# One list for the whole of an attention and MoE kernel: the source orders every engine's work

## The chip, the core and the metric

The kernel runs on one core of one Trainium2 chip. A core has five engines that run side by side, each with its own stream of instructions in a fixed order: TensorE (PE) multiplies matrices, VectorE (DVE), ScalarE (ACT) and GpSimd (POOL) compute element by element, and SyncE (SP) issues most of the DMA transfers. An instruction starts when its engine has finished the ones ahead of it and when the semaphores that it waits for are set; whatever stands behind a waiting instruction on its engine waits too. The metric is the device time of one execution in microseconds (us).

## The reference

Attention over 9 blocks of 64 positions, where a position sees its own block and those before it, and then a feed-forward layer with a squared ReLU on the 4608 tokens of all 8 batches:

```python
def _attn_ref(q, k, v):                      # each (8, 8, 576, 64): batch, head, position, width
    scale = 1.0 / np.sqrt(D)
    scores = scale * np.matmul(q, k.transpose(0, 1, 3, 2))
    mask = block_i >= block_j                # blocks of 64 positions
    scores = np.where(mask, scores, -1000000000.0)
    scores = scores - np.max(scores, axis=-1, keepdims=True)
    attn = np.exp(scores)
    attn = attn / (np.sum(attn, axis=-1, keepdims=True) + 1e-09)
    return np.matmul(attn, v).astype(np.float32)

def _moe_ref(x, w_in, w_out):                # (4608, 512), (512, 2048), (2048, 512)
    h = x @ w_in
    r = np.maximum(h, 0.0)
    return ((r * r) @ w_out).astype(np.float32)
```

All inputs and outputs are fp32. Most matmuls of the kernel run on pairs of fp16 numbers: each operand is scaled by a power of two and split into a high half and the remainder (the low half), and a product is the sum of three matmuls, high by high, high by low and low by high.

## The kernel before

**Attention.** Work is cut into 40 *passes*; most names carry batch, head pair and a number of a row group, so `px_4_2_0_0` is a value product of batch 4, head pair 2. Two heads are always worked on together. Passes 0 to 7 are the rows 0 to 2 of the blocks of batches 0 and 1 (G_X), passes 8 to 15 are rows 3 to 8 of the same (G_Y), and passes 16 to 39 are all rows of batches 2 to 7 (G_XY, three score groups each). Passes 0 to 15 take their scores from fp32 matmuls. The rest first run a *front* (passes 12 to 15 only its part on v): the sums of |q|, |k| and |v| on ACT, two small matmuls (`pm`) that bring the maximum to all partitions, the scales on DVE, and then the split of q and k on ACT and DVE (`qs`, `k1`, and `k2` with the halves swapped), which three DMA transposes turn into `qT` and `kT`. A score group is a set of matmuls into `ps`, a running maximum on DVE, the exponential on ACT (`p32`), its sum on POOL, the reciprocal on DVE, and the scaled split into `p_rows` (high half on ACT, low half on DVE). DMA transposes turn `p_rows` into `p_turned`; in passes 0 to 11 matmuls into `pt` and a copy do it, and the copies of passes 8 to 11 alternate between ACT and DVE (constant EV). The value matmuls (`px`) multiply `p_turned` by the split `v16`, and ACT writes the result to `x32`.

**MoE.** When all head pairs of a batch's rows are there, the norm of the tokens is formed, and x is scaled and split into `xt`. Twelve *chunks* of 384 tokens follow, in the order 0, 1, 2, 4, 3, 5, 7, 6, 8, 10, 9, 11. A chunk has 16 *units*: 12 matmuls into `ph`, then Relu out of PSUM into `r` on ACT, Square of `r` in place on ACT, the cast of `r` to `hidden`'s high half on DVE, and the remainder on DVE (in chunk 0 mostly on POOL). Then come 3 outputs of 48 matmuls each into `po`, a scaling into `ob` on DVE and the transfer to HBM. `ph` and `po` share a ring of 2 PSUM buffers, `r` has 3 buffers, the score groups 2, and `px`, `pm`, `pt` and the norms 2 together.

**What sets the order.** A class `Queue` stands around each engine. Its line 93 issues every instruction of the kernel, so all groups of the profile have line L93 (L96 after the change) and are told apart by their tiles' names. While `nc.held` is set, `Queue` makes each instruction depend on the one before it on its engine, and so the order in which the source calls them is the order on the engine. Otherwise the tile framework's own scheduler chooses the order from its own simulation.

The *head* of the program (the weights, passes 0 to 11, the norms that chunk 0 needs and the 16 units of chunk 0) is ordered by the class `Plan`, called from `plan_head`. Each task has an engine, a duration in ns, the tasks that it comes after, a rank, and the buffer rings that it takes and frees. `run` simulates the engines: among the tasks that can start on the engine that is free first it takes, within LOOK = 300 ns (100 for ranks of 80 and over), the one with the lowest rank, and calls its function at once, with `nc.held` set. The time of a transfer is 1800 ns plus its bytes at 375 per ns on one wire.

The *body* (passes 12 to 39 and everything else of the MoE) is written by generators in program order, and the framework's scheduler orders it. `one_pass` writes a score group with `softmax`, then pours a number of MoE steps (`pour`, `fill`) that FILL gives per pass, for instance:

```python
            softmax(t, group, ready_rows)
            for g in parts:
                defer(DELAY[0], finish, t, g)
            pour(rate / ng / 2)
            if gi == 0 and i + 1 < len(passes):
                front(passes[i + 1])
```

A step is one unit (`moe_in`) or a quarter of an output (`moe_out`, 12 matmuls). `defer` puts value matmuls off by DELAY[0] = 14 steps, a norm by 6, and `hurry` writes them earlier where a buffer is needed again. The front of a pass is written behind the first score group of the pass before it.

Of the kernel before, what the change touches and what calls it, by code (L numbers as in the profile page):

```python
# [44 lines left out]
EV = ("ACT", "DVE")  # L45
SPIN = 5
NQ_CK = 1
W_FIX = 112
DELAY = (14, 6, 1)
FILL = (14, 6, 7, 7, 10, 10, 9, 7)  # L50
# [4 lines left out]
N0 = 60  # L55
LOADS = "p0 p1 r0 p2 r1 r2 p3 r3 r4 r5 r6 r7 r8 r9 r10 r11 r12 r13 Y0 r14 r15 Y1 z0 z1 z2 z3 z4 z5 z6"
# [64 lines left out]
class Plan:  # L121
# [7 lines left out]
    def add(self, name, queue, ns, after, rank, make, takes=(), frees=(), size=0):  # L129
        assert name not in self.tasks, name  # L130
        self.tasks[name] = (queue, ns, after, rank, make, takes, size)
        for owner, ring in frees:
            self.holders.setdefault((owner, ring), []).append(name)

    def run(self):
# [3 lines left out]
        end, issued, taken = {}, {}, {r: [] for r in self.rings}  # L139
        left = list(tasks)  # L140

        def ready(name):
            queue, _, after, _, _, takes, _ = tasks[name]
            needs = list(after)
            for ring in takes:
                if len(taken[ring]) >= self.rings[ring]:
                    needs += self.holders[taken[ring][-self.rings[ring]], ring]
            if any(n not in end for n in needs):
                return None
            at = [issued[n] if tasks[n][0] == queue else end[n] + self.LAG[tasks[n][0]] for n in needs]  # L150
            return max([free[queue]] + at)

        while left:
            times = [(ready(n), tasks[n][3], n) for n in left]
            times = [x for x in times if x[0] is not None]
            if not times:
                raise RuntimeError(f"stuck: {left[:40]}")
            first = min(times)
            queue = tasks[first[2]][0]
            at, _, name = min(  # L160
                (x for x in times if tasks[x[2]][0] == queue and x[0] <= first[0] + (LOOK if x[1] < 80 else 100)), key=lambda x: (x[1], x[0])
            )
            queue, ns, _, _, make, takes, size = tasks[name]
            left.remove(name)
            for ring in takes:
                taken[ring].append(name)
            free[queue] = at + ns
            end[name] = at + ns
            issued[name] = at + ns + 60
            if size:  # L170
                wire = max(wire, at + 1800) + size / 375
                end[name] = wire
            make()

@with_exitstack
def attention_moe_kernel(ctx: ExitStack, tc: tile.TileContext, qk1, v1, qkt, qk, vm, vt, w_in, w_out, out):
# [101 lines left out]

    def pow2_of_max(st, n, name):

        turned, largest, spread, read = pow2_steps(st, n, name)
        turned()
        largest()
        spread()
        return read()
# [144 lines left out]
    def front(t):  # L430

        u, c = t["u"], t["chunks"]
        if t["whole"]:
            t["es"] = D**-0.5
            return
        v32 = t["v32"][:, :, 0:c, :]
        st = small.tile([P, 3], F32, tag="st", name=f"st_{u}")
        a = 2 if t["native"] else 0
        if not t["native"]:
            raw = t["raw"]  # L440
            qs = p1.tile([P, NJ, P], F16, tag="qs", name=f"qs_{u}")
            k1 = p1.tile([P, NJ, P], F16, tag="k1", name=f"k1_{u}")
            k2 = p1.tile([P, NJ, P], F16, tag="k2", name=f"k2_{u}")
            q3 = raw[:, 0].rearrange("p (j d) -> p j d", d=D)
            k3 = raw[:, 1].rearrange("p (j d) -> p j d", d=D)
            nc.scalar.activation(k1[:, :, 0:D], k3, AF.Abs, accum_out=st[:, 1:2])
            nc.scalar.activation(qs[:, :, 0:D], q3, AF.Abs, accum_out=st[:, 0:1])
        else:
            k2 = p1.tile([P, NJ, P], F16, tag="k2", name=f"k2_{u}")
        rest = k2.rearrange("p j d -> p (j d)")[:, 0 : 10 * D].rearrange("p (h c d) -> p h c d", h=2, d=D)  # L450
        nc.scalar.activation(rest[:, :, 0:c, :], v32, AF.Abs, accum_out=st[:, 2:3])
        m = pow2_of_max(st[:, a:3], 3 - a, u)
        s = scale_of(m, A_ATT, 3 - a, u)
        xsc = small.tile([P, 1], F32, tag="xsc", name=f"xsc_{u}")
        nc.vector.tensor_scalar(xsc, m[:, 2 - a : 3 - a], 2.0 ** (-A_ATT - A_P), None, op0=ALU.mult)
        t["xsc"] = xsc
        if t["native"]:
            t["es"] = D**-0.5
        else:
            es = t["es"] = small.tile([P, 1], F32, tag="es", name=f"es_{u}")  # L460
            nc.vector.tensor_scalar(
                es, m[:, 0:1], m[:, 1:2], -(2.0 ** (-2 * A_ATT)) * D**-0.5, op0=ALU.mult, op1=ALU.mult
            )
            nc.scalar.activation(k1[:, :, 0:D], k3, AF.Copy, scale=s[:, 1:2])
            nc.scalar.activation(qs[:, :, 0:D], q3, AF.Copy, scale=s[:, 0:1])
            nc.vector.scalar_tensor_tensor(
                k1[:, :, D:P], k3, s[:, 1:2], k1[:, :, 0:D], op0=ALU.mult, op1=ALU.subtract
            )
            nc.vector.scalar_tensor_tensor(
                qs[:, :, D:P], q3, s[:, 0:1], qs[:, :, 0:D], op0=ALU.mult, op1=ALU.subtract  # L470
            )
            pairs = [k.bitcast(I32).rearrange("p j (z d) -> p j z d", z=2) for k in (k1, k2)]
# [798 lines left out]
```

## Time and profile before

| what | us |
|---|---|
| median of 3 runs (lowest to highest) | 1064.48 (1063.92 to 1066.38) |
| the profiled execution | 1065.6 |
| its span, first to last instruction | 1063.8 |
| busy: PE / DVE / ACT / POOL | 1014.8 / 714.1 / 645.4 / 82.1 |
| `ph` matmuls, 2304, busy | 407.4 |
| `po` matmuls, 1728, busy | 386.7 |
| first `ph` matmul starts at | 38.81 |
| mean granted TensorE clock | 0.989 of full speed |

The page's first part gives busy time, share of the span and count of each engine (PEld is TensorE's weight load, which runs beside the matmuls). Busy times of matmuls overlap, since they are pipelined: a `ph` matmul has a mean of 331 ns though they follow each other faster. A group of instructions reads as line, engine, operation, output<-input, tile shapes, count, then busy time and mean ns of one, then the engine's idle time just before them and what ended it. A row of the timeline gives start, length, the instructions in a run (x12 is twelve of them), and in brackets an idle time before it with what ended it. A row of the table by stretch gives the stretch, its length, busy time and count of the five engines in the order PE, PEld, DVE, ACT, POOL, and then the granted clock, the busy share of the DMA engines and GB/s.

### The profile page before, as it was taken

Reading aid. Unit: us, or ns where it says so; the run is one execution under the profiler, and the core shown is the slowest. Engines: PE = TensorE matmul, PEld = TensorE weight load, DVE = VectorE, ACT = ScalarE, POOL = GpSimd, SP = SyncE. Lnnn points to the kernel's source line nnn. Section 1 sums busy time; section 2 is a strip of 40 time slices with the busy share of each in tenths; the row PEclk is TensorE's granted clock in tenths of the full one; section 3 lists DMA queues with packets and bytes.
Section 4 is the critical chain, followed back from the end, with each engine's and each line's share of the span. In section 5 each row is a group of like instructions: output and inputs, shape, how many; then the busy total and the mean of one; then the engine's idle time right before and its main releaser. Section 6 shows DMA issues by size and latency. Waiting matters only on the chain.

```text
span 1063.8 us, 18829 instructions
## 1 busy us (share of the span) xinstructions
PE 1014.8 (95%) x6867; PEld 535.7 (50%) x6867; DVE 714.1 (67%) x1942; ACT 645.4 (61%) x1636; POOL 82.1 (8%) x182
## 2 busy tenths in 40 slices
PE   7688999999999999998999999999999999999998
PEld 6344434544554555454455455455455555455553
DVE  6999787768879787777479378777768626232230
ACT  7787585866996687488279278567658515032230
POOL 5535100000000000000000000000000000000000
PEclk9899999999999999999999999998999999999999
DMA  9526355886877888478366757577747120000000
GB/s 358 224 85 221 114 118 114 146 162 146 167 149 155 175 164 151 98 131 153 80 127 129 149 108 145 104 158 134 155 81 132 23 69 1 21 11 10 20 1 30
DMA packets 297053, 125.50 MB, mean 118 GB/s; under 512 B 274944, under 2 KB 283136, under 8 KB 296960
## 3 DMA queue, kind: packets, MB, share of 16 engines
q1 hardware_dynamic: 296960, 124.29, 53.7%
q8 instruction: 54, 0.88, 0.3%
q14 instruction: 39, 0.32, 0.1%
HBM read 47.71 MB, written 9.44 MB: 54 GB/s over the span
## 4 chain that ended last, share of the span: by engine, by line
PE 60%; issue 14%; DVE 12%; DMA 6%; ACT 5%; POOL 1%; SPq 0%; ACTq 0%; POOLq 0%; DVEq 0%
PE po L93 29%; PE ph L93 20%; PE ps L93 6%; PE px L93 4%; DMA p_turned<-p_rows 3%; DVE p_rows L93 2%; DVE w L93 2%; DVE ps L93 2%; ACT p L93 2%; DVE nmx L93 1%; ACT p_rows L93 1%; DMA kT<-k 1%; DVE hidden L93 1%; DVE stw L93 1%; ACT r L93 1%
## 5 line engine op out<-in xcount | busy, mean ns | idle before, releaser
L93 PE MATMUL ph<-xt,w 128*128 128x384 f16 x2304 | 407.4, 331 | 7.7 <-ACT r L93 3.3
L93 PE MATMUL po<-w,hidden 128*128 128x512 f16 x1728 | 386.7, 379 | 1.7 <-ACT r L93 1.7
L93 PEld LDWEIGHTS <-w 128*128 128x128 f16 x2304 | 219.1, 99 | 169.3 <-issue 26.3
L93 PEld LDWEIGHTS <-hidden 128*128 128x128 f16 x1728 | 165.1, 98 | 200.6 <-issue 11.1
L93 ACT ACTIVATE p<-ps,nmx 128x576 f32<-128x576 f32 (+8 forms) x264 | 139.6, 540 | 82.5 <-DVE nmx L93 69.8
L93 ACT ACTIVATE r<-ph 128x384 f32<-128x384 f32 x192 | 92.9, 489 | 136.9 <-PE ph L93 131.8
L93 DVE CUSTOM_DVE_ANT_0 ps<-ps,zero,es 128x256 f32<-128x256 f32 (+8 forms) x216 | 118.6, 552 | 42.5 <-PE ps L93 40.9
L93 DVE SCALAR_TENSOR_TENSOR p_rows<-p,rs,p_rows 128x384 f16<-128x384 f32 (+5 forms) x264 | 127.9, 522 | 18.6 <-ACT p_rows L93 12.6
L93 ACT ACTIVATE p_rows<-p,rs 128x384 f16<-128x384 f32 (+5 forms) x264 | 123.9, 544 | 12.0 <-DMA p_turned<-p_rows 6.5
L93 DVE TENSOR_SCALAR ob<-po,uv 128x512 f32<-128x512 f32 x36 | 28.9, 805 | 132.7 <-PE po L93 132.7
L93 DVE CAST hidden<-r 128x384 f16<-128x384 f32 x192 | 67.1, 352 | 56.5 <-ACT r L93 56.3
L93 ACT ACTIVATE r<-r 128x384 f32<-128x384 f32 x192 | 99.3, 526 | 2.8
L93 DVE TENSOR_TENSOR hidden<-r,hidden 128x384 f16<-128x384 f32 x177 | 96.7, 551 | 2.6
L93 PE MATMUL ps<-kT,qT 128*64 128x64 f16 (+4 forms) x960 | 82.2, 295 | 8.7 <-DMA qT<-qs 4.9
L93 PE MATMUL px<-p_turned,v 128*64 128x384 f16 (+5 forms) x1168 | 77.4, 271 | 8.6 <-DMA p_turned<-p_rows 8.4
L93 POOL TENSOR_SCALAR sm<-sm 128x2 f32<-128x2 f32 (+2 forms) x104 | 30.7, 295 | 697.7 <-ACT p L93 642.3
L93 PEld LDWEIGHTS <-v 128*64 128x64 f16 x1128 | 52.2, 110 | 37.9 <-issue 26.0
L93 PEld LDWEIGHTS <-qT 128*64 128x64 f16 x960 | 45.7, 111 | 43.8 <-issue 26.5
L93 ACT ACTIVATION_READ_ACCUMULATOR p<-ps,nmx 128x1 f32 x264 | 54.1, 205 | 0.0
L93 ACT ACTIVATE x<-px,xsc 128x384 f32<-128x384 f32 (+1 forms) x52 | 26.1, 503 | 36.2 <-PE px L93 33.2
L93 PE MATMUL ps<-qk 64*64 64x512 f32 (+5 forms) x224 | 41.7, 472 | 0.8 <-ACT p L93 0.7
L93 DVE RECIPROCAL rs<-sm 128x2 f32<-128x2 f32 (+2 forms) x104 | 17.2, 166 | 31.6 <-POOL sm L93 30.3
(108 smaller groups left out, 771.6 us busy)
## 6 DMA issues: line engine op xcount, KB each, us to landing
qk<-in_qk SPq DMA_DIRECT2D x24, 576.0 KB, 4.7
out<-ob SPq DMA_DIRECT2D x32, 256.0 KB, 2.0
vraw<-in_vm SPq DMA_DIRECT2D x30, 256.0 KB, 3.6
w<-in_w_out SPq DMA_DIRECT2D x10, 512.0 KB, 5.3
qk<-in_qkt SPq DMA_DIRECT2D x8, 576.0 KB, 3.9
w<-in_w_in SPq DMA_DIRECT2D x8, 512.0 KB, 8.4
hidden<-in_w_in SPq DMA_DIRECT2D x6, 512.0 KB, 10.6
raw<-in_w_out SPq DMA_DIRECT2D x6, 512.0 KB, 6.5
```

What stands on the lines that cost most here:

```text
L93: i = make(*a, **k)
```

## The change

`plan_head` and all generators of the body go. `plan_all` gives every task of the kernel to one `Plan`: loads, weights, passes, fronts, norms, units and outputs. `nc.held` is set throughout, so the framework's scheduler orders nothing any more. The arithmetic and the tiles stay the same, except for the engine of a few copies and casts. In detail:

- Ranks: a pass's tasks have 300 + 100 per pass (+30 per score group, +5 or 6 for its transposes and value matmuls); its front has the rank of the pass before it plus 15; MoE matmuls have 10000 + 1000 per chunk, so they are taken only where nothing else can start on PE; the work behind a unit (Relu, Square, cast, remainder) has 250, ahead of all attention of the body.
- Two allowances are new: a PE task of rank 300 or more counts as ready only MARGIN = 600 ns after what it waits for, and a transfer lands LAND = 300 ns later than before.
- A task may name two engines with a duration each, and the list takes the one that can start first: the cast to `hidden`'s high half (DVE 280 ns or ACT 480), the `p_turned` copies and the `p_rows` scaling of passes 8 to 11. Of the 192 casts 185 now stand on ACT and 7 on DVE. Of the 36 copies to `p_turned` 20 stand on ACT (22 before) and 16 on DVE (14); of the scalings of `p_rows` 266 stand on ACT (264 before) and 22 on DVE (24).
- `front`, the softmax and the norm become dictionaries of single steps; an output is put out in 16 pieces of 3 matmuls instead of 4 of 12.
- The durations are set anew, new rings stand for buffers that the framework watched before, the pool of `sq` has 2 buffers instead of 1, and `r` is a tile of 384 columns instead of 512.

The diff, cut to its core:

```diff
+BEGIN = 300
+FILLER = 10000
+CHAIN = 250
+FRONT = 15
+MARGIN = 600
+LATE = 300
+LAND = 300
...
         def ready(name):
-            queue, _, after, _, _, takes, _ = tasks[name]
...
+            for q in queues:
+                lag = self.LAG[q] + (MARGIN if q == "PE" and rank >= LATE else 0)
+                at = free[q]
+                for n in needs:
+                    at = max(at, issued[n] if on[n] == q else end[n] + lag)
+                yield at, rank, name, q
...
-        def high():
-            nc.vector.tensor_copy(g[:, 0], box["r"])
+        def high(q):
+            (nc.scalar.copy if q == "ACT" else nc.vector.tensor_copy)(g[:, 0], box["r"])
...
-        def products(f0):
-            if f0 == 0:
+        def products(f):
+            if f == 0:
                 box["po"] = ps_m.tile([P, 512], F32, tag="mm", name=f"po_{ck}_{t}")
...
-    def one_pass(i, t):
...
-    def plan_head():
+    def plan_all():
...
+        def moe(n):
+
+            ck, prev = turn_of[n], turn_of[n - 1]
+            ends = [f"xs{b}_{g}" for b in range(NB) for g in range(2) if place(b, g)[0] == ck]
...
+            rank = FILLER + 1000 * n
+            for f in range(NF):
...
+                add(
+                    f"ph{k}", "PE", 1970, ends + [f"ph{ck}_{f - 1}" if f else f"low0_{f}"] + ([] if ck else [f"low0_{f}"]),
+                    rank + f if ck else early, start, ("mm",), frees=[(ends[0].replace("xs", "xc"), f"xt{min(ck % 3, 1)}")],
+                )
+                r = CHAIN if ck else early
+                add(f"pos{k}", "ACT", 420, [f"ph{k}"], r, step(1), ("r",), frees=[(f"ph{k}", "mm")])
+                add(f"sqr{k}", "ACT", 440, [f"pos{k}"], r, step(2))
+                add(f"top{k}", {"DVE": 280, "ACT": 480}, 0, [f"sqr{k}"] + over, r, step(3))
...
+                    add(
+                        f"po{ck}_{m}_{f}", "PE", 652, after, rank + 100 + 100 * m + f,
+                        (lambda f=f, box=box: box["s"][0](f)) if f else start, () if f else ("mm",),
+                    )
...
+        for t in passes[WHOLE:]:
...
+            base = BEGIN + 100 * (i - WHOLE)
+            front_rank = base - 100 + FRONT if i > WHOLE else BEGIN - 10
...
+                add(f"tq{i}", "SP", 1350, [f"ql{i}"], r, go("q_turn"), ("qT",), frees=[(f"fq{i}", "qs")], size=9 * block)
...
+            for gi, (group, whole_sets, parts) in enumerate(t["groups"]):
+                k, rank = f"{i}_{gi}", base + 30 * gi
+                row_steps(t, k, group, rank, ready_rows, slots, behind)
...
+                    add(
+                        f"G{i}_{g}", "PE", 1700 if g else 340, back + [f"vl{i}"], rank + 6, lambda t=t, g=g: products(t, g), ("x",),
+                        frees=[(f"vh{i}", "v16")] if g else [],
+                    )
...
-    plan_head()
...
+    plan_all()
```

Two places show what moves. The first is TensorE's order around the first value matmuls of the pass 4_2, which wait for `p_turned`. A row is line, operation, output<-inputs by tile name, and the shape; in front of a matmul stands its weight load. Before:

```order
L93 MATMUL ps_4_3_0_7_6087<-kT_4_3_0_5631,qT_4_3_0_5630 64x128
L93 LDWEIGHTS v16_4_2_0_5275
L93 MATMUL px_4_2_0_0_6041<-p_turned_85,v16_4_2_0_5275 64x192
...
L93 LDWEIGHTS qT_4_3_0_5630
L93 MATMUL ps_4_3_0_7_6087<-kT_4_3_0_5631,qT_4_3_0_5630 64x128
L93 LDWEIGHTS ones_bf_80
L93 MATMUL pm_5_0_0_5978<-dg_5_0_0_5983,ones_bf_80 128x3
...
L93 LDWEIGHTS w1_96
L93 MATMUL ph_3_11_5854<-xt_3_3925,w1_96 128x384
```

And now:

```order
L96 MATMUL ps_4_3_0_7_6049<-kT_4_3_0_5974,qT_4_3_0_5981 64x128
L96 MATMUL pm_5_0_0_6067<-ident_89,st_5_0_0_6006 3x128
L96 LDWEIGHTS hidden_98
L96 MATMUL po_3_1_5994<-w2_97,hidden_98 128x512
...
L96 LDWEIGHTS v16_4_2_0_5625
L96 MATMUL px_4_2_0_0_6094<-p_turned_85,v16_4_2_0_5625 64x192
```

Before, the value matmuls `px_4_2_0_0` stood inside the second score group of pass 4_3 (`ps_4_3_0_7`), with a `pm` matmul of the next front between the group's last ones and unit 11 of chunk 3 behind. Now the score group is whole, and matmuls of an output of chunk 3 (`po_3_1`) stand between it and the value matmuls.

The second is ACT's order around units 6 to 8 of chunk 3. Before:

```order
L93 ACTIVATE r_3_6_5669<-r_3_6_5669 128x384
L93 ACTIVATE k1_5_0_0_5973,st_5_0_0_5971<-qk32_5_0_0_5872 128x9x64
L93 ACTIVATE p_rows_84<-p32_4_2_0_7_5737,rs_4_2_0_7_5743 128x512
L93 ACTIVATE r_3_7_5766<-ph_3_7_5753 128x384
L93 ACTIVATE qs_5_0_0_5972,st_5_0_0_5971<-qk32_5_0_0_5872 128x9x64
L93 ACTIVATE k2_5_0_0_5974,st_5_0_0_5971<-vraw0_82 128x640
L93 ACTIVATE r_3_8_5784<-ph_3_8_5771 128x384
L93 ACTIVATE p32_4_2_0_8_5823,sm_4_2_0_8_5824<-ps_4_2_0_8_5807,nmx_4_2_0_8_5820 128x576
L93 ACTIVATE r_3_7_5766<-r_3_7_5766 128x384
L93 ACTIVATE r_3_8_5784<-r_3_8_5784 128x384
```

And now:

```order
L96 ACTIVATE r_3_6_5582<-ph_3_6_5546 128x384
L96 ACTIVATE r_3_6_5582<-r_3_6_5582 128x384
L96 CAST hidden_98<-r_3_6_5582 128x384
L96 ACTIVATE p_rows_84<-p32_4_1_0_7_5399,rs_4_1_0_7_5448 128x384
L96 ACTIVATE r_3_7_5603<-ph_3_7_5568 128x384
L96 ACTIVATE r_3_7_5603<-r_3_7_5603 128x384
L96 CAST hidden_98<-r_3_7_5603 128x384
L96 ACTIVATE p_rows_84<-p32_4_1_0_7_5399,rs_4_1_0_7_5448 128x128
L96 ACTIVATE v16_4_2_0_5625<-vraw0_82,s_4_2_0_5421 128x640
L96 ACTIVATE r_3_8_5629<-ph_3_8_5589 128x384
L96 ACTIVATE r_3_8_5629<-r_3_8_5629 128x384
L96 CAST hidden_98<-r_3_8_5629 128x384
```

Before, Relu (`r_3_7<-ph_3_7`) and Square (`r_3_7<-r_3_7`) of unit 7 had two sums of the next front, the Relu of unit 8 and two exponentials between them. Now Relu, Square and the cast to `hidden` of a unit stand together, with one or two rows of attention between two units.

More of the change, by code (lines that the diff above doesn't have):

```diff
@@ L130, in add @@
         assert name not in self.tasks, name
-        self.tasks[name] = (queue, ns, after, rank, make, takes, size)
+        if not isinstance(queue, dict):
+            queue = {queue: ns}
+        self.tasks[name] = (queue, after, rank, make, takes, size)
         for owner, ring in frees:
@@ L146, in ready @@
                 if len(taken[ring]) >= self.rings[ring]:
[L147 to L155, printed above, removed]
+                    for n in self.holders[taken[ring][-self.rings[ring]], ring]:
+                        if n not in end:
+                            return
+                        needs.append(n)
@@ L577, in inverse, with spread @@
             nc.vector.reciprocal(rs, box["sm"])
-        def spread():
+        def spread(q="DVE"):
             if short:
@@ L1078, in part_steps @@
-            add(f"low{k}", "DVE", 610, [f"cast{k}"], rank, lambda: box["s"][3]())
-        def row_steps(t, gi, group, rank, after, short, y):
-            k = t["key"] + (f"_{gi}" if y is not None else "")
-            w = sum(D * (j + 1) for j, _ in group)
-            n = len(group)
+            last = [f"low{wi}_{f - 1}"] if f else []
+            if wi and not f:
+                last += [f"join{v}_{g}" for v in range(2) for g, at in PLACES[v].items() if at == ("w2", 0)]
+            add(f"bits{k}", "POOL", 740, [raw], early + 10, lambda: low_bits(raws[wi][f]))
@@ new lines, in part_steps, with row_steps @@
+            add(f"prelu{k}", "ACT", 610, [raw] + ["A5"] * (f == NF - 1), early, start, takes)
+            add(
+                f"join{k}", "DVE", 660, [f"prelu{k}", f"bits{k}"] + hold, early, lambda: box["s"][1](),
+                frees=frees + [(f"prelu{k}", tag)],
+            )
+            add(f"cast{k}", "ACT", 640, [f"join{k}", f"w{wi}e"] + last, rank, lambda: box["s"][2]())
+            add(f"low{k}", "DVE", 760, [f"cast{k}"], rank, lambda: box["s"][3](), frees=ends)
+        def row_steps(t, k, group, rank, after, frees, parts):
+            w, n, i = width(group), len(group), t["i"]
+            short = i < NT * NHP
@@ L1084, in row_steps @@
             box = {}
             def start():
-                box["s"], _ = rows(t, group)
+                box["s"], box["b"] = rows(t, group)
                 box["s"]["score"]()
             get = lambda name: lambda: box["s"][name]()
-            add(f"A{k}", "PE", fp32(w) + 40 * n * 2, after, rank + (3 if short else 0), start, ("s",),
-                frees=t["raw_of"])
-            add(f"B{k}", "DVE", exact(w) + 70 * n + 100, [f"A{k}"], rank + (2 if short else 0), get("largest"))
-            wait = [f"E{t['i'] - SLOTS}"] if short and t["i"] >= SLOTS else []
@@ L1095, in row_steps @@
-            add(f"C{k}", "ACT", exact(w) + 160 * n + 75, [f"B{k}"] + wait, rank + (2 if short else 0), get("raised"),
-                () if short else ("p32",), frees=[(f"A{k}", "s")])
+            late = 2 if short else 0
+            score = 1.7 * w + 80 * n if t["native"] else 0.84 * w + 40
+            largest = 1.05 * w + 100 * n + 100 if t["native"] else 1.07 * w + 130 * n
+            add(f"A{k}", "PE", score, after, rank + (3 if short else 0), start, ("s",), frees=frees)
+            add(f"B{k}", "DVE", largest, [f"A{k}"], rank + late, get("largest"))
@@ L1113, in plan_head @@
+        done = {}
+        counts = [[min(4, j // 2 + 1 - c) for j, _ in g for c in range(0, j // 2 + 1, 4)] for g, _, _ in G_Y]
         sq = {}
```

729 lines of the change are left out of this document (406 added, 323 removed).

## The prediction

> **What bounds the kernel now.** I read the page's first part, then busy time by stretch, what TensorE waited for, and the places themselves.
>
> ```profile
> PE 1014.8 (95%) x6867; PEld 535.7 (50%) x6867; DVE 714.1 (67%) x1942; ACT 645.4 (61%) x1636; POOL 82.1 (8%) x182
> ...
> 0.00:45.00 45.00, 30.65 (x263) 21.61 (x264) 34.82 (x95) 30.68 (x92) 25.77 (x49) 0.92 0.91 344
> 45.00:110.00 65.00, 57.06 (x351) 29.47 (x349) 63.06 (x134) 49.34 (x107) 29.50 (x39) 0.97 0.40 137
> 110.00:850.00 740.00, 716.95 (x5109) 375.08 (x5108) 552.80 (x1582) 513.64 (x1336) 26.86 (x96) 0.99 0.66 130
> 850.00:1064.00 214.00, 210.11 (x1150) 109.55 (x1148) 63.41 (x132) 51.70 (x101) 0.00 (x0) 1.00 0.08 21
> ```
>
> The columns after the stretch are its length, then PE, PEld, DVE, ACT and POOL busy, the granted clock, DMA share and GB/s. TensorE sets the time: it is idle 1063.8 - 1014.8 = 49.0 us. Of these 14.35 lie before 45 us, 7.94 from 45 to 110 (there DVE is busy 63.06 of 65, so DVE sets the pace), 23.05 in the long middle, and 3.9 at the end, where the last output leaves. The same matmuls run after the change, so an order can only win TensorE's idle time, what follows from it, and what matmuls lose at switches. In the middle, TensorE waits for:
>
> ```profile
> PE px L93 <- DMA p_turned<-p_rows: 8.4, 7, 2.1
> PE ps L93 <- DMA qT<-qs: 4.9, 4, 2.2
> PE ph L93 <- ACT r L93: 3.3, 5, 1.4
> PE ps L93 <- DMA kT<-k: 3.3, 4, 2.0
> PE po L93 <- ACT r L93: 1.7, 2, 1.2
> ```
>
> That is 21.6 of the 23.05 us (total, times, longest). They are waits for the next matmul in a fixed order, while MoE matmuls that could run stand behind it:
>
> ```profile
> 480.72 1.00 PE L93 MATMUL ps<-kT,qT 128*64 128x512 f16 x10
> 483.61 0.27 PE L93 MATMUL px<-p_turned,v 128*64 128x192 f16 x2 [1.88 <-DMA p_turned<-p_rows]
> 483.69 0.22 PE L93 MATMUL ps<-kT,qT 128*64 128x128 f16 x1
> ```
>
> Two value matmuls stand inside a score group and hold it 1.88 us, with 12 matmuls of ph ready behind.
>
> **The change, term by term.** For distances in the new order I need rates, from the undisturbed tail and two groups of the middle:
>
> ```profile
> 966.75 31.08 PE po L93 x144
> 997.83 31.20 PE ph L93 x192
> ...
> 248.48 1.91 PE L93 MATMUL px<-p_turned,v 128*64 128x384 f16 x30
> 251.44 1.06 PE L93 MATMUL ps<-kT,qT 128*64 128x512 f16 x12
> ```
>
> A ph matmul takes 31.20/192 = 0.1625 us, a po matmul 0.216, a score group about 1.0, the 42 value matmuls of a pass about 2.4.
>
> *Waits of the middle.* For the pass at 483.6 (4_2) the work in TensorE's order between its second score group and its first value matmul was six ph units, 28 value and 38 score matmuls: 6 x 1.95 + 1.8 + 2.8 = 16.3 us, and it waited. In the new order 48 ph, 75 po, 42 value and 40 score matmuls stand there: 7.8 + 16.2 + 2.4 + 2.9 = 29.3 us. I counted so for all 24 passes from 2_0 on. The five that waited there had 12.7 to 19.2 us before; the new order gives 19.6 to 59.5. From the third group to the second value part the three that waited had 12.4 to 16.1; now 19.8 to 56.3. From the second pm matmul (which frees the scaling of q and k, their split and three transposes) to the first scores the six that waited had 9.1 to 13.0; now 9.7 to 23.1, four of them under 11 (9.7, 9.7, 10.4, 10.9). So px waits should go except for late transposes:
>
> (all p_turned transposes, issue to landing)
>
> ```profile
> DMA to landing us min/median/max: 3.7/4.3/8.6
> ```
>
> A p_turned transpose 4.3 us over its median has no cover where the list places its user on the median. I keep 3 us for these (about one such landing), 1 us for each of the four tight fronts, 2 us for waits on ACT: 9 of 23.05 us. Gain 14 us; bounds 23 (all go) and 0 (each goes elsewhere).
>
> *The clock behind the waits.*
>
> ```profile
> 370.62 1.33 PE L93 MATMUL ps<-kT,qT 128*64 128x320 f16 x14 [2.04 <-DMA kT<-k]
> 371.88 3.16 PE L93 MATMUL ph<-xt,w 128*128 128x384 f16 x12
> ...
> 370.60:374.00 3.40, 3.38 (x21) 2.19 (x21) 1.94 (x8) 3.36 (x9) 0.34 (x1) 0.50 1.31 257
> 496.90:500.30 3.40, 3.40 (x22) 1.78 (x22) 1.80 (x3) 3.40 (x9) 0.19 (x1) 0.50 0.16 65
> 718.80:722.20 3.40, 3.40 (x13) 1.57 (x12) 1.97 (x7) 0.79 (x5) 0.29 (x1) 0.50 1.14 211
> 739.20:742.60 3.40, 3.40 (x19) 1.75 (x16) 3.37 (x11) 2.22 (x6) 0.00 (x0) 0.51 0.89 170
> ```
>
> After a wait of 2.04 us the granted clock is 0.50 for 3.4 us and twelve ph matmuls take 3.16 us. Four such stretches cost half their length each, 6.8 us. I expect two to remain: gain 3.4; bounds 0 and 6.8. [...]
>
> *Switches.*
>
> ```profile
> 197.55 2.12 PE L93 MATMUL ph<-xt,w 128*128 128x384 f16 x12
> 199.60 1.10 PE L93 MATMUL px<-p_turned,v 128*64 128x384 f16 x19
> 200.80 2.11 PE L93 MATMUL ph<-xt,w 128*128 128x384 f16 x12
> 203.55 2.11 PE L93 MATMUL ph<-xt,w 128*128 128x384 f16 x12 [0.64 <-ACT r L93]
> ```
>
> Twelve ph matmuls before a switch start 199.60 - 197.55 = 2.05 us ahead of the next kind, against 1.95 in the tail: 0.10 us at a switch. Runs of one kind in TensorE's order, ph and po counted as one kind, fall from 551 to 422. MoE runs alone fall by 47 (205 to 158): 47 x 0.10 = 4.7; all 129 give 12.9. Many of the lost ones are pairs of matmuls of under 0.2 us, so I take 6; bounds 4 and 13.
>
> *The casts that move.* hidden's high half is cast on DVE 192 times; the list lets an engine be chosen and puts 185 of them on ACT.
>
> ```profile
> L93 ACT ACTIVATE r<-r 128x384 f32<-128x384 f32 x192 | 99.3, 526 | 2.8
> L93 DVE CAST hidden<-r 128x384 f16<-128x384 f32 x192 | 67.1, 352 | 56.5 <-ACT r L93 56.3
> ...
> L93 ACT ACTIVATE r<-ph 128x384 f32<-128x384 f32 x129 | 62.2, 489 | 23.2 <-PE ph L93 18.7 <-DVE hidden L93 2.8 <-DVE mx L93 1.3
> ...
> L93 ACT ACTIVATE wt<-w 128x512 f32<-128x512 f32 x18 | 12.0, 676 | 3.6 <-DVE w L93 1.8 <-DMA w<-in_w_out 1.7
> ...
> 28.14 1.25 ACT L93 ACTIVATE wt<-w 128x512 f32<-128x512 f32 x2
> ```
>
> No row has this cast on ACT; the nearest, the same shape, is 526 ns (below it lies DVE's 352). ACT gains 185 x 0.526 = 97 us, DVE loses 65. In the middle (the third row) 129 units run, so ACT goes from 513.6 to about 513.6 + 129 x 0.526 = 581 of 740 us. It lies beside TensorE's work as long as three ACT instructions of a unit (489 + 526 + 526 = 1.54 us) and the attention work queued between fit in the time from one ph unit to the next, 1.95 us plus what stands between. In the new ACT order I added the rows between each two units' first ACT instruction, each 0.1 us under its mean since rows overlap at their ends (two wt rows of 0.676 take 1.25): in each chunk from the second on ACT falls at most about 1.1 us behind TensorE and catches up, less than one unit, and two PSUM buffers cover that. In the old order the same sum reaches 8 us. I cost it at 0; without that cover it is the third rival. [...]
>
> *The head.*
>
> ```profile
> L93 DVE TENSOR_SCALAR p_rows<-p,rs 128x576 f32<-128x576 f32 (+5 forms) x24 | 10.6, 483 | 0.3
> L93 DVE COPY p_turned<-pt 128x512 f32<-128x512 f32 (+3 forms) x14 | 7.7, 548 | 3.7 <-PE pt L93 3.7
> ```
>
> In chunk 0 DVE loses 12 casts and two scalings and gains two copies: 12 x 0.352 + 2 x 0.483 - 2 x 0.548 = 4.1 us by means, 3 with the overlap, where DVE sets the pace. Two fp32 score groups also move ahead of the first ph unit, into idle time; but weight joins move ahead of x on DVE. I take 3; bounds -4 (first ph unit later) and 10.
>
> *Sum.* 14 + 3.4 + 6 + 3 = 26.4 us off the profiled execution. It took 1065.6 us (span 1063.8 plus 1.8 around it): 1039.2. It lay 1.1 over the median of the runs, 1064.48, so I predict **1038 us**.
>
> **The rivals.**
> 1. *All waits go.* The distances above speak for it, the 8.6 us landing and four tight fronts against it. 23 + 6.8 + 10 + 8 = 48: 1017 us. Chance 0.15.
> 2. *The waits only move.* The list plans each transfer with one duration, and places attention matmuls as soon as they should be ready, ahead of all MoE work; each late transfer is then a wait of about the old size. For it speaks the landing's spread; against it that the old order waited where distances were short. Only switches and head remain, 6 + 3: 1056 us. Chance 0.18.
> 3. *ACT becomes the bound of the ph stretches: slower.* For it speaks how full ACT is where the 16 ph units of a chunk run (here those of chunk 3):
>
> ```profile
> 450.00:500.00 50.00, 45.90 (x371) 25.50 (x370) 37.58 (x117) 39.41 (x107) 1.35 (x7) 0.97 0.82 150
> ```
>
> 39.4 of 50 us, and 16 x 0.526 = 8.4 more make 47.8, with hardly a gap for work that comes in bursts. The old waits on ACT cost 3.3/5 = 0.66 us each; at 40 of the 129 units they eat the 26.4 us, and from there it is slower. At half of them, 65 x 0.66 = 43 us: 1081 us. Against it: the sums in the new ACT order. [...] Chance 0.10.
> 4. *No change.* Waits on ACT at about 40 units, or a head 4 us later with the waits moved, cancel the rest: 1064 us. Chance 0.05.
>
> **How the numbers follow.** Main case 0.52; its own range, from half the wait gain to nearly all with clock, is 1027 to 1048. Two in ten outside leaves out the better half of rival 1 and nearly all of rivals 3 and 4: 1018 to 1060. About 0.2%, 2.1 us, is what a measurement here can tell from no change. Faster: 0.52 + 0.15 + 0.18 = 0.85; same 0.05; slower 0.10.
>
> **What would show it.** Right: PE idle in the middle under 12 us with px waits under 4 us; at most two stretches of clock 0.50 after 110 us; casts of hidden on ACT at 0.45 to 0.55 us each; the wait of ph for ACT not above 4 us; twelve ph matmuls at 1.95 to 2.05 us. Wrong: ph waiting for ACT in total over 20 us (rival 3), px and ps waits near 16 us again (rival 2), or a first ph unit later than 43 us.

## The result, and the profile after

| | before | changed |
|---|---|---|
| median of 4 runs, us | 1064.2 (1063.14 to 1066.38) | 1030.7 (1029.62 to 1031.21) |
| profiled execution, us | 1065.6 | 1029.6 |
| its span, us | 1063.8 | 1027.8 |

The ratio is 0.9681, with a 95% interval of 0.9664 to 0.9699: 33.5 us faster by the medians, 36.0 by the two profiled spans. The first part of the page after, its table by stretch (the same columns as before the change, the last stretch shorter), and TensorE's waits between 110 and 850 us:

```profile
PE 996.2 (97%) x6867; PEld 535.1 (52%) x6867; DVE 690.8 (67%) x1757; ACT 747.3 (73%) x1821; POOL 82.4 (8%) x182
```

```profile
0.00:45.00 45.00, 32.77 (x272) 22.99 (x273) 34.90 (x90) 29.98 (x90) 27.52 (x48) 0.96 0.91 343
45.00:110.00 65.00, 57.52 (x356) 30.98 (x355) 63.00 (x124) 58.73 (x130) 29.44 (x37) 0.96 0.37 131
110.00:850.00 740.00, 731.79 (x5313) 390.41 (x5310) 557.98 (x1484) 594.26 (x1475) 25.48 (x97) 1.00 0.65 134
850.00:1028.00 178.00, 174.10 (x932) 90.67 (x929) 34.93 (x62) 64.34 (x127) 0.00 (x0) 1.00 0.04 14
```

```profile
PE ps L96 <- DMA kT<-k: 3.7, 4, 1.8
PE pm L96 <- DVE dg L96: 1.0, 2, 0.5
...
PE px L96 <- DMA p_turned<-p_rows: 0.8, 2, 0.4
```

TensorE is idle 1027.8 - 996.2 = 31.6 us, 17.4 less than before. By stretch that is 12.23 us (14.35 before), 7.48 (7.94), 8.21 (23.05) and 3.7 at the end (3.7; the last row of each table ends about 0.2 us after the last instruction, which makes it 3.9). Between 110 and 850 us the waits of px are 0.8 us in place of 8.4, those of ps for a transpose 3.7 in place of 8.2, and no wait of ph for ACT is left. The granted clock of the third stretch is 1.00: not one half-clock stretch is left between 113 and 850 us, where there were four.

The other half of the gain is busy time: 1014.8 - 996.2 = 18.6 us for the same 6867 matmuls. To see where it had been lost I took, from 110 us on, each matmul's start to the next one's start, without idle time, less the rate of its kind (the rates of the prediction). The sum over pairs of one kind is near zero in both traces. What remains stands in the half-clock stretches and at changes of kind:

| from 110 us to the end | before | changed |
|---|---|---|
| in half-clock stretches, us | 6.3 | 1.0 |
| changes of kind in the trace | 505 | 380 |
| at changes of kind, us | 36.4 | 24.4 |
| pairs of one kind, us | -0.7 | -2.5 |

(Here each of ph, po, ps, px, pm and the rest is a kind of its own; the order's count of 551 and 422 took ph and po as one and the whole program.) The place of the prediction in the new kernel, the first two score groups of pass 4_3 and the first value matmuls of 4_2 (the last row), and below it a switch in the pass before:

```profile
485.11 0.33 PE L96 MATMUL ps<-kT,qT 128*64 128x320 f16 x2
486.13 1.64 PE L96 MATMUL ps<-kT,qT 128*64 128x320 f16 x26 [0.70 <-DMA kT<-k]
487.70 0.27 PE L96 MATMUL pm<-ident,st 128*3 128x128 f32 x1
487.81 1.46 PE L96 MATMUL po<-w,hidden 128*128 128x512 f16 x6
489.20 0.53 PE L96 MATMUL px<-p_turned,v 128*64 128x192 f16 x12
...
455.55 2.12 PE L96 MATMUL ph<-xt,w 128*128 128x384 f16 x12
457.61 1.06 PE L96 MATMUL ps<-kT,qT 128*64 128x512 f16 x12
```

No value matmul stands inside a score group any more, and the value matmuls of 4_2 no longer wait. The scores of 4_3 now wait 0.70 us for their own transpose, two matmuls into the first group. Twelve ph matmuls still start 2.06 us ahead of the next kind (457.61 - 455.55), as before.

### The profile page after: what moved, and what is told of

Same layout as the page of the kernel before. It is cut to its first block, busy times and chain, and to the rows that moved or that the text cites. A ratio compares the mean times of both kernels' runs of the same rounds, so it can differ in the third digit from the quotient of the medians.

```text
span 1027.8 us, 18835 instructions
## 1 busy us (share of the span) xinstructions
PE 996.2 (97%) x6867; PEld 535.1 (52%) x6867; DVE 690.8 (67%) x1757; ACT 747.3 (73%) x1821; POOL 82.4 (8%) x182
## 5 line engine op out<-in xcount | busy, mean ns | idle before, releaser
L96 PE MATMUL ph<-xt,w 128*128 128x384 f16 x2304 | 390.6, 327 | 4.9 <-ACT w L96 1.6
L96 DVE CUSTOM_DVE_ANT_0 ps<-ps,zero,es 128x320 f32<-128x320 f32 (+8 forms) x216 | 120.1, 556 | 43.6 <-PE ps L96 38.5
L96 ACT ACTIVATE p_rows<-p,rs 128x448 f16<-128x448 f32 (+6 forms) x266 | 128.6, 539 | 22.4 <-DVE rs L96 17.0
L96 DVE SCALAR_TENSOR_TENSOR p_rows<-p,rs,p_rows 128x128 f16<-128x128 f32 (+5 forms) x264 | 127.5, 524 | 12.6 <-ACT p_rows L96 10.3
L96 ACT CAST hidden<-r 128x384 f16<-128x384 f32 x185 | 94.6, 512 | 6.5 <-DVE w L96 0.7
L96 PE MATMUL ps<-kT,qT 128*64 128x320 f16 (+4 forms) x960 | 72.1, 289 | 4.4 <-DMA kT<-k 3.7
L96 PE MATMUL px<-p_turned,v 128*64 128x384 f16 (+5 forms) x1168 | 71.8, 270 | 0.8 <-DMA p_turned<-p_rows 0.8
L96 PEld LDWEIGHTS <-qT 128*64 128x64 f16 x960 | 43.5, 110 | 34.6 <-issue 20.0
L96 DVE TENSOR_REDUCE nmx<-ps 128x1 f32<-128x576 f32 (+5 forms) x72 | 31.3, 479 | 6.3 <-PE ps L96 6.3
```

The lines of the kernel that those rows point to most:

```text
L96: i = make(*a, **k)
```

## The experiments

Each kernel is the changed one with the edit shown, or the one before where it says so; of an edit only the lines that matter are shown. Where the list is run with another table, two value products of a pass may come before the first one's copy, so these kernels also keep the two apart by name; in the run "again" that changes no order. Times are medians of 4 runs, against 1030.7 for the changed kernel; the kernel before had medians of 1060.6 to 1063.4 beside them, on different chips, so for differences of a few us the ratios and their intervals are to be read as well.

**The baseline again.**

> The changed kernel once more, with the same order on every engine, on the chip of the three runs beside it, so that differences of a few us can be read: 1029 to 1032 us by every theory.

1030.86 us, ratio 0.9701 (0.9673 to 0.973). Its profiled execution took 1031.1, with two half-clock stretches more in the head than the one shown above (mean clock 0.991 for 0.995). Its waits for transposes between 110 us and the end:

```profile
PE ps L96 <- DMA kT<-k: 2.4, 5, 0.7
PE px L96 <- DMA p_turned<-p_rows: 2.2, 4, 1.3
```

The total is the same as above (4.6 us for 4.5), its parts are not: the same order gave 3.7 and 0.8 there. So a difference of about 1.4 us in one of these rows tells nothing yet.

**The casts on DVE alone.**

```diff
-                add(f"top{k}", {"DVE": 280, "ACT": 480}, 0, [f"sqr{k}"] + over, r, step(3))
+                add(f"top{k}", {"DVE": 280}, 0, [f"sqr{k}"] + over, r, step(3))
```

> The changed kernel, but the list may put the cast to hidden's high half on DVE alone, as before the change. Theory: the casts on ACT cost nothing and win nothing, the list's order is what counts. Then the time moves only by what the new list's order brings: 18 fewer runs of one kind on TensorE (404 for 422) at 0.11 us are -2 us, and the shortest way from a front's second pm matmul to its scores grows from 9.7 to 11.5 us, which may take 1 to 2 us of the kT waits (3.7 us): 1027 to 1031 us, ph waiting for DVE or ACT under 2 us in the middle. Rival: the free choice of the engine is itself a source of the gain. Then DVE, 65 us busier, falls behind, ph or po waits for DVE hidden by more than 5 us, and the time is over 1036.

1025.9 us, ratio 0.9664 (0.9618 to 0.971): 5 us faster than the changed kernel by the medians, better than either theory had it; the intervals of the ratios overlap. Its first part, and three of TensorE's waits between 110 and 850 us:

```profile
PE 992.2 (97%) x6867; PEld 534.1 (52%) x6867; DVE 745.2 (73%) x1938; ACT 662.1 (65%) x1640; POOL 82.2 (8%) x182
```

```profile
PE px L96 <- DMA p_turned<-p_rows: 1.4, 2, 1.0
PE ph L96 <- ACT r L96: 1.2, 1, 1.2
...
PE ps L96 <- DMA kT<-k: 0.5, 1, 0.5
```

The rival is out: DVE takes 54 us more and TensorE waits no longer than before. That the choice of the engine costs nothing is in doubt too; the second pair below has to settle it. Of the 4.8 us between the two spans, 4.0 are TensorE's busy time (no half-clock stretch behind 110 us, the clock between 110 and 850 us is 1.00, 19 changes of kind fewer, shorter pairs) and only 0.8 its idle time: the waits for kT are down from 3.7 to 0.5, and other waits came in their place.

**Score groups cut in two.** A task on an engine of its own that takes no time stands between the halves, so that an allowance passes and MoE matmuls come between:

```diff
-            add(f"A{k}", "PE", score, after, rank + (3 if short else 0), start, ("s",), frees=frees)
+                add(f"A{k}", "PE", 0.84 * part1 + 20, after, rank, start, ("s",))
+                add(f"gap{k}", "GAP", 0, [f"A{k}"], rank, lambda: None)
+                add(f"A2{k}", "PE", 0.84 * (w - part1) + 20, [f"gap{k}"], rank, lambda: box["s"]["score"](cut), frees=frees)
```

> The changed kernel with each score group of the passes from 16 on cut into two tasks on TensorE, with MoE matmuls forced between them: the same matmuls, 94 more runs of one kind (516 for 422), the shortest ways to the transposed operands unchanged (9.7, 18.5, 19.4 us). Theory: each run of one kind costs about 0.11 us at its end (11.5 us won by 103 fewer runs in the body): 94 x 0.11 = 10 us more, 1039 to 1043 us, with TensorE busy by about 10 us more and idle as before. Rival: switches cost nothing by themselves, and the busy time that TensorE lost was something else (waits too short to be seen, DMA traffic): 1030 to 1033 us.

1034.27 us, ratio 0.9747 (0.9707 to 0.9788). Its first part, and one cut group in the timeline:

```profile
PE 1002.6 (97%) x6867; PEld 528.2 (51%) x6867; DVE 688.7 (67%) x1758; ACT 748.1 (72%) x1820; POOL 81.4 (8%) x182
```

```profile
453.48 0.68 PE L96 MATMUL ps<-kT,qT 128*64 128x512 f16 x8
454.09 2.12 PE L96 MATMUL ph<-xt,w 128*128 128x384 f16 x12
456.15 0.57 PE L96 MATMUL ps<-kT,qT 128*64 128x448 f16 x4
```

The same matmuls take 6.4 us more of TensorE's busy time, so changes of kind do cost, and the rival's 0 is out. Counted as in the table above, changes rise from 380 to 474 and what is lost at them from 24.4 to 34.4 us: 10.0/94 = 0.106 us each, the theory's price. The time rose by only 3.6 us, between the ranges of the theory and of the rival: 1.5 of the 10 come back inside the score groups (the pairs that were cut there count no longer), 1.0 in a half-clock stretch that the cut order doesn't have, 1.2 ahead of 110 us, and TensorE's idle time is 1.7 us less. So the price of a change was right, and the sum over the kernel was not.

**No allowances.**

```diff
-MARGIN = 600
+MARGIN = 0
...
-LAND = 300
+LAND = 0
```

> The changed kernel with both allowances at 0 (600 ns ahead of a TensorE task, 300 ns on a landing). Theory: the waits went because MoE matmuls stand between a transpose's source and its user for longer than the landing takes; the allowances are a small part of that. The shortest ways to px are 15.7 and 16.1 us (the old order waited at 12.1 to 19.2), to the scores 9.0: px waits 1 to 3 us, ps waits 4 to 7, no more than one stretch at half clock, 8 runs fewer (-0.9): 1029 to 1035 us. Rival: the allowances are what removed the waits; then px and ps together wait 12 us or more in the middle, with two or more half-clock stretches: 1038 us and over.

1036.49 us (1033.71 to 1037.03), ratio 0.9757 (0.9716 to 0.9798). The profiled execution is the fastest of the four. Its waits between 110 and 850 us:

```profile
PE pm L96 <- DVE dg L96: 2.9, 8, 0.6
PE px L96 <- DMA p_turned<-p_rows: 2.8, 5, 1.2
PE ps L96 <- DMA kT<-k: 2.4, 5, 1.0
PE ps L96 <- DMA qT<-qs: 1.5, 4, 0.5
```

And the middle in the table by stretch:

```profile
110.00:850.00 740.00, 726.98 (x5290) 387.96 (x5286) 553.07 (x1476) 595.12 (x1473) 24.49 (x97) 1.00 0.66 134
```

px and ps wait 6.7 us for transposes (4.5 with the allowances), in 14 short waits, and in this execution no half clock follows. The other three had a mean clock of 0.992 to 0.993 where this one had 0.997, so theirs was lower somewhere; where isn't on record. This is the theory's mechanism, 1.5 us above its range by the median. The allowances are worth 3 to 6 us. TensorE's idle time in the middle is 740 - 726.98 = 13.0 us without them, so of the fall from 23 to 8 us the list's order brought about two thirds and the allowances at most a third.

**A list that thinks transfers faster than they are** (and has no allowance).

```diff
-MARGIN = 600
+MARGIN = 0
...
-LAND = 300
+LAND = -2500
```

> The changed kernel with a list that takes transfers to land 2.8 us sooner than the changed kernel's list does (LAND -2500 for 300) and with no allowance ahead of TensorE. Theory: a matmul waits for a transposed operand where less work than the chain needs stands between source and user. The shortest ways from a front's second pm to its scores fall from 9.7 to 6.4, 6.5, 6.8, 7.8 us, below the 9.1 to 13.0 at which the old order waited; those to px from 19.6 to 13.6: the waits of ps for qT and kT come back with 8 to 25 us in all, px with 2 to 8, and with them three to six stretches at half clock: 1042 to 1062 us. Rival: the old waits came with the old order's clusters of transfers and not with short ways; then waits stay under 8 us: 1030 to 1036 us.

1111.06 us, ratio 1.0471 (1.0422 to 1.0519): slower than the kernel before.

TensorE's waits between 110 and 850 us:

```profile
PE px L96 <- DMA p_turned<-p_rows: 16.7, 13, 2.2
PE ps L96 <- DMA qT<-qs: 13.1, 11, 2.3
PE ps L96 <- DMA kT<-k: 12.5, 12, 1.7
```

The old waits are back, 42.3 us for transposes in 36 waits of about the old size, with six stretches at half clock from 180 us on (the clock between 110 and 850 us is 0.99). The run without allowances differs from this one by the landings alone. The six fronts with the shortest ways from their second pm matmul to their scores (6.3 to 8.2 us, counted in the trace by the prediction's rates) all wait, 1.9 to 2.4 us each. The theory's direction holds and its size falls short by far: TensorE's idle time went from 31.6 to 1102.3 - 1011.9 = 90.4 us, and its busy time rose by 15.7. My explanation for the rest is argued, not shown: with every engine's order fixed, a transpose that lands late holds TensorE, the groups behind it on DVE and ACT begin late, and the next transposes start late too.

**Transfers planned 1.2 us later.**

```diff
-LAND = 300
+LAND = 1500
```

> The changed kernel with a list that takes transfers to land 1.2 us later (LAND 1500 for 300). Theory: what is left of the waits (ps for kT 3.7 us, of it one of 1.8) comes from fronts whose scores stand 9.7 to 10.9 us behind their pm; the shortest are now 11.0, 11.0, 11.0, 11.6 us, and runs of one kind fall by 11 (-1 us): kT and qT waits under 1.5 us, 1025 to 1029 us. Rival: these waits are single late landings that no common allowance meets, and the longer lead delays others: 1030 to 1034 us.

1029.9 us, ratio 0.9693 (0.9664 to 0.9723): no change that can be told.

The largest waits between 110 and 850 us:

```profile
PE pm L96 <- DVE dg L96: 2.1, 2, 1.7
PE ps L96 <- DMA kT<-k: 2.1, 1, 2.1
```

Four kT waits became one of 2.1 us, and a half-clock stretch of 6.8 us came (from 424 us). The time lies between the two ranges; that one long wait is left fits the rival's account.

**Both: casts on DVE and transfers planned later.** The edits of the two runs together.

> The changed kernel with the cast to hidden's high half on DVE alone and landings 1.2 us later in the list. It is to the run with the later landings alone (1029.9 us) what the run with the cast on DVE was to the changed kernel. Theory now: the casts on ACT did cost, some 4 to 5 us, since ACT's attention work stands behind them and arrives later; then this pair shows it again: 1022 to 1027 us. The shortest ways to the scores are 12.9 us, to px 20.4 (both above every way at which a wait was seen in the old order but a few), so kT, qT and px waits together under 2 us; 406 runs of one kind. Rival: the 5 us were chance of one order, and the casts cost nothing: 1028 to 1031 us.

1021.32 us, ratio 0.961 (0.9591 to 0.9629), the fastest kernel of the study: 9.4 us faster than the changed one, a little below the theory's range, and 8.6 faster than the run with the later landings alone, where the list may choose the engine of the casts. The pair repeats the sign of the first one (5 us) with a larger size, and here the intervals of the ratios are apart (0.9591 to 0.9629 against 0.9664 to 0.9723). So the list does worse with the choice than without it in two tables, by 5 to 9 us. It is not shown that this is the cost of a cast on ACT itself: both pairs also change TensorE's order (404 runs of one kind for 422, 406 for 411), and no run kept that order. First part and the largest waits behind 110 us:

```profile
PE 991.7 (97%) x6867; PEld 534.5 (52%) x6867; DVE 743.7 (73%) x1935; ACT 660.3 (65%) x1643; POOL 80.3 (8%) x182
```

```profile
PE pm_w L96 <- DVE rs L96: 1.0, 1, 1.0
PE ph L96 <- ACT r L96: 0.9, 1, 0.9
```

No wait for a transpose (kT, qT, p_turned) is left in its list of waits above 0.2 us, and no half clock between 110 us and the end of the work. The pairs don't win in the same place. The first won nearly all of it in busy time; here 4.5 of the 8.0 us between the spans are idle time, and most of the other 3.5 are the half-clock stretch of the run with the later landings, which is gone. The middle of that run, and of this one:

```profile
110.00:850.00 740.00, 729.03 (x5304) 390.61 (x5299) 556.20 (x1481) 595.08 (x1475) 25.40 (x98) 1.00 0.67 134
...
110.00:850.00 740.00, 734.14 (x5355) 393.71 (x5352) 600.87 (x1621) 537.56 (x1359) 24.66 (x98) 1.00 0.67 134
```

**Later still.**

```diff
-LAND = 300
+LAND = 2700
```

> The changed kernel with the casts on DVE alone and landings 2.4 us later in the list than in the changed kernel (2700 for 300). The series of landings at -2500, 300 and 1500 has measured 1111, 1031 and 1030 us with the casts on either engine, and 1026 and 1021 us at 300 and 1500 with the casts on DVE. Theory: once the ways to the scores are above 11 to 13 us, at which the last waits were seen, more lead wins nothing (they are now 14.5 us and over, those to px 22 us), and no wait for a transpose is left that it could take: 1019 to 1024 us, kT, qT and px waits under 1 us. Rival: a longer lead holds buffers longer and delays the norms that open a chunk: 1025 us and over.

With the casts on DVE: 1024.12 us, ratio 0.9659 (0.9641 to 0.9677), just above the theory's range, and slower than the run with 1500 (that interval ends at 0.9629). The waits for transposes are gone, and what is left is of other kinds:

```profile
PE ps L96 <- ACT p L96: 1.7, 4, 0.7
PE pt L96 <- DVE m_w L96: 1.2, 1, 1.2
```

So more lead wins nothing once these waits are gone, and here it cost about 3 us by the medians.

**Outputs in pieces of 12 matmuls**, as before the change.

```diff
-                for f in range(NF):
+                for f in range(0, NF, PIECE):
...
-                        f"po{ck}_{m}_{f}", "PE", 652, after, rank + 100 + 100 * m + f,
+                        f"po{ck}_{m}_{f}", "PE", 652 * PIECE, after, rank + 100 + 100 * m + f,
```

> The changed kernel with outputs in pieces of 12 matmuls, as before the change, in place of 3. Theory: 13 fewer runs of one kind (409 for 422) at 0.11 us are -1.4 us; attention waits up to 1.9 us longer for a piece to end, which costs TensorE nothing since the piece is its own work; ways to the scores 10.4 us, the shortest to px 14.5: 1028 to 1031 us. Rival: fine pieces are what lets attention in at once and keeps the chain fed: 1033 us and over, with waits of ps and px.

1028.27 us, ratio 0.9673 (0.9656 to 0.969): 2.4 us faster by the medians, at the theory's lower end, and not told apart by the ratio. Fine pieces are not what brought the gain.

> The changed kernel with all three edits: casts on DVE, landings 1.2 us later, outputs in pieces of 12. 388 runs of one kind (422 in the changed kernel): -34 x 0.11 = -3.7 us by the price of a switch; the shortest ways are 12.2 and 21.1 us, so 2 us of its 8 us of waits in the middle go, and the extra 1 us that the casts on ACT cost beside that: 1021 to 1025 us. Rival: a floor is reached at the run with the casts on DVE: 1025 to 1029 us.

All three together: 1023.08 us (1020.2 to 1023.71), ratio 0.9619 (0.9599 to 0.9639). Its 18 runs of one kind fewer than the run with the first two edits (388 for 406) bring nothing that can be told from it.

**The work behind a unit ranked last.**

```diff
-CHAIN = 250
+CHAIN = 20000
```

> The changed kernel with the work behind a unit (Relu, Square, cast, remainder, scaling of the output) ranked behind all attention (20000 for 250). Theory: the added casts stay free because the list puts a unit's work on ACT ahead of attention. With it last, Relus come late, TensorE waits for the two PSUM buffers of ph and po, the list moves attention ahead instead, and the ways to the scores fall to 4.8 to 8.8 us: ps waits over 10 us, ph for ACT r or po for DVE over 5: 1036 to 1055 us. Rival: the rank doesn't matter, since the list sees every engine and TensorE always finds something: 1028 to 1034 us.

1101.68 us, ratio 1.0368 (1.0338 to 1.0398): slower than before the change.

TensorE's waits behind 110 us, and the middle in the table by stretch:

```profile
PE ph L96 <- ACT r L96: 46.4, 22, 6.3
PE px L96 <- DMA p_turned<-p_rows: 7.4, 9, 1.5
...
PE ps L96 <- DMA kT<-k: 0.8, 2, 0.6
```

```profile
110.00:850.00 740.00, 678.00 (x4836) 355.91 (x4833) 540.60 (x1464) 541.79 (x1368) 26.41 (x97) 0.97 0.63 128
```

The theory had the direction, not the place: the scores don't wait (0.8 us), the ph units wait for their buffers, 2 us each time on average (46.4 us in 22 waits), and the granted clock of the stretch is 0.97, for 1.00 in the changed kernel. That the units don't fall behind on ACT, as I counted it, hangs on this one rank, which also moves the remainder and the scaling of the output on DVE.

**The kernel before, with the casts on ACT.** Its scheduler orders it.

```diff
         def high():
-            nc.vector.tensor_copy(g[:, 0], box["r"])
+            (nc.scalar.copy if ck else nc.vector.tensor_copy)(g[:, 0], box["r"])
```

> The kernel before, with the cast to hidden's high half on ACT for chunks 1 to 11 and nothing else changed (the scheduler orders it as before). Theory: the casts are free only in an order that keeps ACT's work of a unit together. In the old order ACT, 92 us busier, falls behind: ph waits for ACT r by 8 to 20 us (5 us before), the fronts' ways to the scores are down to 6.2 to 7.2 us and their waits rise from 8 to 12 or more; 30 fewer runs give back 3 us: 1068 to 1085 us. Rival: moving the cast off DVE is itself a gain, whatever the order: under 1060 us.

1100.59 us, ratio 1.0367 (1.0325 to 1.0409): 36 to 39 us slower than before.

TensorE's waits between 110 and 850 us:

```profile
PE px L93 <- DMA p_turned<-p_rows: 15.7, 17, 1.7
PE ps L93 <- DMA qT<-qs: 9.5, 7, 2.8
PE nq L93 <- DVE sq L93: 5.0, 4, 1.9
PE ph L93 <- ACT r L93: 4.3, 7, 1.2
```

The rival (the move is a gain in itself) is out. The theory had the cost too low and its main share in the wrong place: ph's wait for ACT is 4.3 us (3.3 before), while px and qT waits are about double. For the fronts the trace shows why, and it is the theory's second part. From a front's second pm matmul to the landing of its last kT transpose it takes no longer than before (median 11.7 us, 12.5 before). But the scheduler, given another engine for the cast, made another order: in 11 of the 24 fronts the way to the scores is now 5.8 to 9.0 us, where 9.1 was the shortest. Why px waits longer I did not follow up.

## Why the prediction was right

The predicted time was 1038 us, the measured one 1030.7, inside the main case's own range (1027 to 1048). Step by step, with the span's 36.0 us:

- **Waits of the middle: 14 us forecast, 14.8 measured** (23.05 to 8.21). The distances carried it: the ways of 19.6 us and over to px left 0.8 us of waits (2.2 in the run "again"). Of the 3 us kept for late p_turned landings 2 were too many; the slowest transpose of `p_rows` took 6.0 us from issue to landing, not 8.6. The 2 us for ACT were not needed for ph, and about as much went to small waits of pm, pt and others. The four tight fronts at 1 us each agree with the 3.7 us in four waits for kT by luck. Counted in the new trace by the same rates, these waits stand at fronts with ways to the scores of 9.7, 11.2, 12.9 and 16.5 us, so three of the four tight fronts don't wait at all. The longest wait, 1.80 us, stands at the way of 12.9, and in the run "again" the same place waits 0.64. That short ways make the waits is shown by the run with faster planned landings, and rival 2's mechanism is real there; among ways of 10 to 17 us their length alone doesn't tell which front waits.
- **The clock: 3.4 us forecast, 6.3 measured** in the four stretches that went (6.8 by half their length). "I expect two to remain" failed: none did. A wait of 1.80 us was left, and no half clock followed it (1.00 in the 3.4 us from 757.7 us on). The step that failed took each wait near 2 us as a danger by itself; the last section shows a longer wait than these with no half clock behind it.
- **Switches: 6 us forecast, about 12 measured** (36.4 to 24.4 us at changes of kind). The price of 0.10 us was right; the discount was wrong ("many of the lost ones are pairs of matmuls of under 0.2 us, so I take 6"). 12.0 us over 125 fewer changes are 0.096 us each, short runs included, so the upper bound of 13 was the sum to take.
- **The casts: cost forecast 0; with the choice of their engine the list is 5 to 9 us slower.** In the changed profile a cast takes 0.512 us (forecast 0.526), and ACT gains 747.3 - 645.4 = 101.9 us. The group of the casts, and the table by stretch for the ph units of chunk 3:

```profile
L96 ACT CAST hidden<-r 128x384 f16<-128x384 f32 x185 | 94.6, 512 | 6.5 <-DVE w L96 0.7
```

```profile
430.00:465.00 35.00, 34.90 (x288) 20.98 (x284) 24.93 (x70) 33.67 (x86) 0.68 (x4) 1.00 0.75 159
```

  Where ph units run, ACT is busy 33.67 of 35 us and TensorE is still busy 34.90, so the point that I worked out, that the units don't fall behind, holds. What I left out is the rest of the order: the choice moves the attention work on ACT too, and with it what the list places on TensorE. Which of these costs is open. The fronts, whose transposes would leave late behind a busier ACT, are the first suspect, and the kT waits look like it (3.7 against 0.5 us, 2.1 against none). The traces don't bear it out: from a front's second pm matmul to the landing of its last kT transpose it takes a median of 12.4 us in the changed kernel and 13.7 with the casts on DVE, and 12.5 and 13.1 in the second pair. Ahead of the longest kT wait ACT kept the split of k waiting for 3.1 us, with exponentials and `p_rows` and not one cast. Here the list of tasks with its casts on VectorE is the better one by those 5 to 9 us, though ACT never became the bound.
- **The head: 3 us forecast, 2.6 less idle time before 110 us.** The first ph unit starts at 41.72 us, 2.9 later than before, with 11.2 us of idle time ahead of it in place of 14.1; from there to 110 us it is 8.5 us in place of 8.2. So the gain lies ahead of the first ph unit, where two score groups moved into idle time, and none shows behind it, where DVE was to be relieved: the size came out, the reason given for it did not.

The sum came out 9.6 us of span short: 2.9 for the clock and 6 for the switches, with 0.8 on the waits and -0.4 on the head. The other 0.3 are 1.8 in pairs of one kind, -1.0 in the half-clock stretch that now ends behind 110 us, and -0.5 of busy time ahead of it. What the choice of the engine costs lies inside these terms: without it they would have been 5 to 9 us larger. So the time is closer to the forecast than the steps deserve: gains taken too small and a cost left out partly cancel, and that is luck. Rival 1, with everything gone (1017 us), was reached by no kernel; the best run, at 1021, has its waits for transposes gone, and 5.9 us of other idle time in the middle, the head and its switches are left. Rival 3, ph waiting for ACT, needs another order: the run with the unit's work ranked last shows it, with 46.4 us of such waits and 1102 us.

## What to carry to other kernels

An order written out for the whole program is worth what its landing times and ranks are worth: the same list with landings planned 2.8 us earlier and no allowance, or with the buffer-freeing work ranked last, is slower than the kernel before, while landings planned 1.2 us later cost nothing that can be told. Price every change of kind on TensorE, short runs too (about 0.1 us each here). Of work moved to an engine with room, ask not only whether its own consumer waits; run the other choice too, since the list makes another order of everything else. Idle time of TensorE costs itself, and at times clock behind it: the half clock, 0.50 for 3.4 us, came here behind waits of 2.04 and 2.33 us and not behind one of 2.81 us.

## What the runs showed of the hardware

I had taken the half clock as following a single wait of about 2 us. The traces show something else: a wait of 2.81 us in the old order with the casts on ACT is followed by none. Its row and that of a wait of 2.33 us in the timeline of that kernel, and the table by stretch for the time around both:

```profile
601.22 0.54 PE L93 MATMUL ps<-kT,qT 128*64 128x320 f16 x4 [2.33 <-DMA qT<-qs]
...
692.76 0.54 PE L93 MATMUL ps<-kT,qT 128*64 128x320 f16 x4 [2.81 <-DMA qT<-qs]
```

```profile
687.70:691.10 3.40, 2.25 (x16) 1.20 (x15) 3.36 (x11) 3.40 (x9) 0.19 (x1) 1.00 0.61 118
691.10:694.50 3.40, 1.74 (x12) 0.94 (x13) 3.40 (x11) 3.40 (x9) 0.00 (x0) 1.00 1.10 203
694.50:697.90 3.40, 3.40 (x26) 1.62 (x24) 3.37 (x4) 3.40 (x10) 0.00 (x0) 1.00 1.14 209
...
599.00:602.40 3.40, 1.18 (x8) 0.50 (x9) 3.31 (x6) 3.40 (x11) 1.72 (x1) 1.00 1.10 207
602.40:605.80 3.40, 3.40 (x10) 1.20 (x9) 1.81 (x4) 3.40 (x9) 0.00 (x0) 0.50 1.34 133
```

Around the wait of 2.81 us the granted clock stays 1.00, with TensorE busy 2.25 and 1.74 us of the first two stretches of 3.40 us. The stretch with the wait of 2.33 us has TensorE busy 1.18 us, and in the next one the clock is 0.50. So the length of a single wait did not tell whether a half clock followed: behind one of 2.04 us in the kernel before (at 370.62 us) the clock was 0.50 for 3.4 us, behind one of 2.81 us it was not. What decides it is not shown.
